# A table of slots for the side work of the x2 stage, an earlier second scale of w_out2, and a square moved one job back

## Chip, core and metric

The kernel runs on one core of a Trainium2 chip. The metric is the device time of one execution in microseconds (us). Engines: PE (TensorE, matrix products), DVE (VectorE), ACT (ScalarE), POOL (GpSimd), SP (SyncE, which here only issues DMAs; ACT issues some too).

## What is computed

```python
attn = masked softmax(q k^T / 8) v            # 4 x 8 heads, 576 tokens, 64 wide
x = attn as (2304, 512)
a, b = x @ w1, x @ w2                         # 512 -> 1024
x2 = ((a * b) @ w3) @ w_out                   # -> 512
h = x2 @ w_in                                 # 512 -> 2048
out = where(h > 0, h, exp(min(h, 0)) - 1) @ w_out2     # -> 512
```

All in float32 within the reference's tolerance; the kernel works with pairs of reduced-precision numbers (a high part and what it leaves over, the low part), so one product of the reference is three on PE.

## The kernel before

**Stages.** Attention, with the products a = x w1 and b = x w2 of the first three batches, is ordered by a planner and is the same in both kernels. Then, in program order: the a and b products of the last batch (`run_unit(ab_unit(...))`, L697); M = w3 w_out in eight units (`m_unit`, L1090); the **x2 stage**, x2 = M^T g (L1387); and the **last stage**, h and out (L1545 and L1495).

**Order.** Outside attention nothing is scheduled: each engine runs its instructions in the order in which the Python code emits them. An instruction that waits holds up all that stands behind it on its engine, and the same holds for the queues on which SP and ACT issue DMAs.

**Weights** come as 64-bit words in chunks of 128x2048 int32 (1 MB). A chunk's conversion (`conv_ops`) is: `top` (ACT, L337), `rest` (DVE, L347), `sign` (DVE, L351), `join` (DVE, L354), and for w_in and w_out2 a `square` with a sum per partition (ACT L370, or DVE L372) from which a power-of-two scale follows (`root`, L996 and L999). After `sign` the raw buffer is free and ACT issues the load of the chunk after next (L322). A w_out2 chunk (`wo_steps`) then is scaled (ACT, L1049), copied to its high half (ACT, L1050), and its low half is formed (POOL, L1051). These conversions are cut into `jobs`, and `run_jobs(k)` runs the next k of them at given places of the a·b, M, x2 and last stages.

**x2 stage.** Six passes x of 384 tokens, each of four blocks e: 24 blocks n = 4x + e of 24 matrix products each, into one of four PSUM banks. ACT evicts each block (L1425 for two passes, L1428 into one of two `x2s` buffers for the others, which SP stores) and squares it (L1225). All passes use the same eight split tiles `sl`. Right after the products of a pass's last block, n = 3, 7, 11, 15, 19, eight `split_g` are emitted, each an ACT copy (L326) and a DVE subtraction (L327), which refill them for the next pass; a refill waits for the products that read the old contents, and the first products of the next pass wait for the refill.

**Beside x2** a table `slot[n]`, run at the end of block n, holds the work on w_in, four pairs of chunks q: two conversions with square (`conv`), four sums of quarters on POOL (`both`, L1293), and then either seven products of the scaled quarters (`direct`, one ACT copy L1315 and one DVE subtraction L1318 each; q = 0, 1) or seven stores to DRAM (`all_out`, q = 2, 3). Before, pair q takes slots 5q to 5q+4, and the directs 5q+6 to 5q+9. The squares of a pair are added over partitions by a small PE product (`total`, L1229) at n = 5q+5, whose result DVE reads one block later (`w_scale`). Sums and scalings of x2's first two passes (`sums`, `high_b`, `low_b`) stand in passes 2 and 3.

**Last stage.** Three groups p of tokens by eight f: 24 steps s. A step has seven products (`product`, L1545) into two PSUM banks, whose results DVE and ACT combine (L1571, L1586) into four quarters, on which the ELU is formed and scaled by a column of `c_by` (L1477, L1482); between the products PE is filled with output products of the step before (L1495). For the first four steps the scale of w_out2 comes from half of its chunks; then all eight chunks are known, and a second maximum over partitions is taken through DRAM (`everywhere`: store, L1006, load into `mxb`, L1010, DVE reduction, L1013). In step 3 the maximum per partition is taken after product 4 (L1625), the load is emitted after product 6, and in step 4 after product 1 DVE reads it, computes `shift` and overwrites `c_by` (`h_scale`, L1260 to L1264).

## Time and profile before

| | |
|---|---|
| median of 3 runs | 1009.46 us (1007.98 to 1011.92) |
| profiled execution, its own time | 1010.8 us |
| its span, first to last instruction | 1009.0 us |
| busy: PE, DVE, ACT, POOL | 948.3, 760.4, 572.1, 408.7 us |
| mean granted PE clock | 0.986 |
| attention with its a·b products | 0 to about 430 us |
| last a·b products | to about 468 us |
| M | about 469 to 515 us |
| x2 stage | 514.9 to 637.5 us |
| last stage | 637.5 to 1009.0 us |

Busy shares are means over stages that have different limits. An idle stretch of PE is named by what released it; what it costs is read in the stage where it lies. The granted clock is that of PE, 1.00 being 2.4 GHz and 0.50 being 1.2 GHz.

### The profile page before, as it was taken

What the parts mean: (1) busy time and instruction counts of PE and PEld (TensorE: products, weight loads), DVE (VectorE), ACT (ScalarE), POOL (GpSimd) and SP (SyncE); (2) the same over time, 40 slices, a digit from 0 to 9 for tenths busy, and PEclk for the clock granted to TensorE, in tenths of its full rate; (3) what the DMA queues carried; (4) which work ended last, traced back from release to release, by engine and by line L of the source; (5) the groups of instructions that cost most, each with busy time, mean ns of one, the idle gap of its engine ahead of it and who ended that gap; (6) DMA issues with size and microseconds to landing.
All of it is one profiled execution on the core that took longest, in us unless ns stands there. A gap on an engine that the chain in (4) does not pass through costs nothing. (4 is left out here: it accounts for less than half of the span.)

```text
span 1009.0 us, 17082 instructions
## 1 busy us (share of the span) xinstructions
PE 948.3 (94%) x6086; PEld 697.7 (69%) x6086; DVE 760.4 (75%) x1445; ACT 572.1 (57%) x1003; POOL 408.7 (41%) x553
## 2 busy tenths in 40 slices
PE   7889999999899999998999979799899999999998
PEld 4456788978889988997888968454455555555554
DVE  6889886988677777586846985599769666776664
ACT  5777776887567765355456564666446223543333
POOL 3478774888688976252402322356300000000000
PEclk9999999999999999999999988999999999999999
DMA  8446655566999888775745556531001200010001
GB/s 265 150 130 164 154 154 157 150 175 167 201 176 204 180 165 161 223 255 176 267 132 172 187 192 202 204 106 34 17 1 44 82 1 1 1 63 1 1 1 63
DMA packets 158866, 130.58 MB, mean 129 GB/s; under 512 B 117340, under 2 KB 145468, under 8 KB 154172
## 3 DMA queue, kind: packets, MB, share of 16 engines
q1 hardware_dynamic: 154668, 99.82, 37.5%
q10 hardware_dynamic: 4112, 29.66, 8.9%
q8 instruction: 48, 0.79, 0.3%
q14 instruction: 38, 0.31, 0.1%
HBM read 80.68 MB, written 21.05 MB: 101 GB/s over the span
## 5 line engine op out<-in xcount | busy, mean ns | idle before, releaser
L697 PE MATMUL ab<-x,W 128*128 128x256 f32 (+1 forms) x1536 | 224.7, 299 | 5.5 <-DVE g L712 3.3
L697 PEld LDWEIGHTS ab<-x,W 128*128 128x128 f32 x1536 | 209.1, 190 | 14.0 <-issue 6.0
L1495 PE MATMUL o<-WO,gg 128*128 128x512 f16 x864 | 213.7, 380 | 0.0
L1545 PE MATMUL h<-so,WI 128*128 128x384 f16 x1008 | 193.2, 329 | 11.0 <-ACT th L1586 5.7
L1545 PEld LDWEIGHTS <-WI 128*128 128x128 f16 x1008 | 99.4, 99 | 96.0 <-issue 15.6
L1571 DVE SCALAR_TENSOR_TENSOR th<-h,back,th 128x384 f32<-128x384 f32 x168 | 100.9, 614 | 79.8 <-PE h L1545 74.7
L1495 PEld LDWEIGHTS <-gg 128*128 128x128 f16 x864 | 84.7, 98 | 85.2 <-issue 0.8
L537 DVE SCALAR_TENSOR_TENSOR e<-s,st,e 128x576 f32<-128x576 f32 x144 | 115.2, 809 | 24.5 <-ACT e L531 22.9
L1387 PE MATMUL x<-sl,M 128*128 128x384 f32 x576 | 110.6, 353 | 9.7 <-DVE sl L327 6.2
L513 DVE TENSOR_REDUCE st<-s 128x1 f32<-128x576 f32 x144 | 106.1, 750 | 17.7 <-PE s L503 10.1
L548 POOL TENSOR_TENSOR hl<-e,hl 128x512 f16<-128x512 f32 x94 | 110.1, 1172 | 21.4 <-ACT hl L544 17.1
L1387 PEld LDWEIGHTS x<-sl,M 128*128 128x128 f32 x576 | 106.3, 198 | 12.6 <-DVE sl L327 8.3
L1472 ACT ACTIVATE et<-et 128x384 f32<-128x384 f32 x96 | 49.1, 511 | 107.9 <-DVE et L1471 107.9
L1477 ACT ACTIVATE gg<-th,c_by 128x384 f16<-128x384 f32 x96 | 59.0, 614 | 81.1 <-DVE th L1475 81.1
L531 ACT ACTIVATE e<-s,st 128x576 f32<-128x576 f32 x108 | 78.4, 737 | 25.4 <-POOL st L521 16.4
L503 PE MATMUL s<-qk 128*128 128x288 f32 x480 | 82.7, 305 | 7.2 <-DVE e L537 6.3
L503 PEld LDWEIGHTS s<-qk 128*128 128x128 f32 x480 | 67.5, 188 | 16.0 <-issue 9.6
L544 ACT ACTIVATE hl<-e 128x576 f16<-128x576 f32 x94 | 63.2, 681 | 22.6 <-DMA pt<-hl 12.0
L1475 DVE SCALAR_TENSOR_TENSOR th<-et,th 128x384 f32<-128x384 f32 x96 | 56.5, 589 | 6.9 <-ACT et L1472 6.2
L1482 DVE SCALAR_TENSOR_TENSOR gg<-th,c_by,gg 128x384 f16<-128x384 f32 x96 | 60.2, 627 | 0.2 <-ACT gg L1477 0.2
L491 PE MATMUL s<-qkp 128*64 128x288 f32 x288 | 42.4, 429 | 7.1 <-ACT pt L589 3.7
L1090 PE MATMUL m<-WO,w 128*128 128x512 f32 x192 | 44.4, 391 | 3.0 <-DVE M L1100 1.9
(153 smaller groups left out, 1351.9 us busy)
## 6 DMA issues: line engine op xcount, KB each, us to landing
rqk<-in_qk SPq DMA_DIRECT2D x24, 576.0 KB
raw_wo<-in_wo ACTq DMA_DIRECT2D x12, 1024.0 KB
th<-g_dr SPq DMA_DIRECT2D x48, 192.0 KB
raw_w<-in_w SPq DMA_DIRECT2D x8, 1024.0 KB
raw_w<-in_w3t ACTq DMA_DIRECT2D x8, 1024.0 KB
raw_win<-in_win ACTq DMA_DIRECT2D x8, 1024.0 KB
vr<-in_v SPq DMA_DIRECT2D x16, 320.0 KB
g_dr<-g SPq DMA_DIRECT2D x16, 320.0 KB
```

The lines of the kernel that those rows point to most:

```text
L503: T.matmul(s[:, n, :HS], q, k[:, c:c + HS], start=(x == 0), stop=(x == len(ops) - 1))
L513: V.tensor_reduce(st[i][:, 0:1], sc[i][:, :, :HS], axis=AX.XY, op=ALU.max if plain else ALU.min, negate=plain)
L531: A.activation(et[i], sc[i][:, :, :HS], AF.Exp, bias=st[i][:, k:k + 1], scale=esc if plain else -1.0)
L537: V.scalar_tensor_tensor(et[i], sc[i][:, :, :HS], st[i][:, 1:2], et[i], op0=ALU.is_ge if p < NPL else ALU.is_le, op1=ALU.mult, accum_out=s ...
L544: A.activation(hl[i][:, :S], et[i].rearrange("p a b -> p (a b)"), AF.Copy)
L548: G.tensor_tensor(t[:, S + 64:], e[:, :512], t[:, :512], op=ALU.subtract)
L697: T.matmul(o[:, :w], wf[:, m, wx, kt, :], x[:, xx, :], start=(kt == 0 and k == 0), stop=(kt == NK - 1 and k == 2),)
L1387: T.matmul(o[:, :TB], M[:, f, mx, e * P:(e + 1) * P], gh[j, f][:, gx, :], start=(k == 0), stop=(k == 23),)
L1482: V.scalar_tensor_tensor(h[:, 1, :], x, c["by"], h[:, 0, :], op0=ALU.mult, op1=ALU.subtract)
L1495: T.matmul(po[j, t], dst["h"][:, gx, t * P:(t + 1) * P], WO[f // 2 % 4][:, f // 8, f % 2, wx, :], start=(first and k == 0), stop=(stop and ...
L1545: T.matmul(o[:, :TB], w[:, wx, kt, :], bs[k][:, kt, xx, :], start=(i == 0), stop=(i == 5),)
L1571: V.scalar_tensor_tensor(x, a, bk, b, op0=ALU.mult, op1=ALU.add)
```

## The change

Four edits.

1. A w_out2 chunk becomes five jobs instead of four: the square leaves the job of its join and starts the next, `size`; scaling and copying (`halves`) are a job of their own. The M stage runs `4 + f % 2` jobs per unit instead of 4.
2. The table beside x2 is rewritten. Pair q's two conversions and its sums stand at slots `t0[q]`; slots 2, 6, 10, 14 and 18 are empty. `directs` stand at 5, 7, 9 and 11; the stores of q = 2 and 3 at 13 and 17; `total` for pair q at n = 4, 8, 12, 16. `sums`, `high_b` and `low_b` go to slots 13 to 20. Of the last 20 w_out2 jobs, 10 run in slots 16 to 22 (before: 4 of 16 in slots 19 to 23).
3. In the last stage the remaining jobs run in steps 0 to 2, four per step (before: steps 0 to 3, three per step); `high_b` of the last two operands is emitted in step 0.
4. The second scale goes into columns of its own, `c_late`: maximum in step 2 after product 5, load emitted in step 3 after product 2, read and `h_scale` in step 3 after product 5 (for the other two groups in step 5).

```diff
         def size():
+            ops[7](raw_[:, c], A)
             root(two[:, c], raw_[:, c], LEAST, 2.0 ** -13)
...
-        return [
-            [ops[0], ops[1], lows], [ops[2]], [ops[3], lambda: ops[7](raw_[:, c], A)], [size, halves]
-        ]
+        return [[ops[0], ops[1]], [ops[2]], [ops[3]], [size], [halves] + [lows] * (q % 4 < 2)], lows
...
         if f < 6:
-            run_jobs(4)
+            run_jobs(4 + f % 2)
...
-        at = 5 * q
-        for i, ops in enumerate((ca, cb)):
-            for n, fns in enumerate(conv(keys[i], ops, i)):
-                slot[at + 2 * i + n] += fns
-        slot[at + 4].append(both)
+        def conv(i):
+            ops = (ca, cb)[i]
+            for fn in ops[:3]:
+                fn()
+            next_load(keys[i])
+            ops[3]()
...
+        def second():
+            size(0)
+            conv(1)
+            size(1)
+
+        t0 = ((0, 1, 3), (3, 4, 7), (8, 9, 11), (12, 13, 15))[q]
+        slot[t0[0]].append(call(conv, 0))
+        slot[t0[1]].append(second)
+        slot[t0[2]].append(both)
         if q > 1:
-            slot[at + 5].append(all_out)
+            slot[t0[2] + 2].append(all_out)
         else:
-            order = (1, 4, 6, 3, 0, 2, 5)
-            for n, k in enumerate(order):
-                slot[at + 6 + n // 2].append(call(direct, k))
-            slot[at + 10].append(lambda: behind.pop(0)())
+            slot[(5, 9)[q]].append(lambda: directs((1, 4, 6, 3)))
+            slot[(7, 11)[q]].insert(0, lambda: directs((0, 2, 5)))
...
-    for n in (19, 20, 22, 23):
-        slot[n].append(lambda: run_jobs(1))
+    for n, k in ((13, 0), (15, 1), (15, 2), (16, 3)):
+        slot[n].append(call(sums, k))
+    for k, n in enumerate((16, 17, 19)):
+        slot[n].append(call(high_b, k, 0))
+        slot[(17, 19, 20)[k]].insert(0, call(low_b, k, 0))
+    for n, k in ((16, 3), (17, 1), (19, 1), (20, 3), (21, 1), (22, 1)):
+        slot[n].append(call(run_jobs, k))
...
-            for q in range(4):
-                if n == 5 * q + 5:
-                    seen = total(o, wm[:, 2 * q:2 * q + 2])
-                    reads.append(lambda q=q, seen=seen: (seen(wg[:, q:q + 1], 1), w_scale(q)))
+            if n in (4, 8, 12, 16):
+                q = n // 4 - 1
+                seen = total(o, wm[:, 2 * q:2 * q + 2])
+                reads.append(lambda q=q, seen=seen: (seen(wg[:, q:q + 1], 1), w_scale(q)))
...
-            lows[q] = elu_low({"x": x, "name": q + "_" + nm, "dst": gg[q], "by": c_by[:, at:at + 1]})
+            lows[q] = elu_low({"x": x, "name": q + "_" + nm, "dst": gg[q], "by": (c_by if s < NH // 2 else c_late)[:, at:at + 1]})
...
-        run_jobs(int(s < NH // 2))
+        run_jobs(int(s < 3))
...
-        if s == NH // 2:
-            seen[1](o_two[:, 1:2])
...
+        if s == 3:
+            seen_o[0]()
...
+        if s == 2:
+            while behind:
+                behind.pop(0)()
+            V.tensor_reduce(o_two[:, 1:2], cols("wo_two", 8), axis=AX.X, op=ALU.max)
+            seen_o = everywhere(o_two[:, 1:2])
+        if s == 3:
+            seen_o[1](o_two[:, 1:2])
+            V.reciprocal(shift, o_two[:, 1:2])
+            V.tensor_scalar(shift, shift, o_two[:, 0:1], None, op0=ALU.mult)
+        if s in (3, 5):
+            h_scale((0,) if s == 3 else (1, 2), o_two[:, 1:2], c_late)
```

Three places in the programs show what moves.

**DVE ahead of the fourth split (n = 15), before.** `w_win_7300` is the second chunk of pair 2, with its square (`u_win_7298`); the `WI` rows are directs of pair 1, the `so` rows `low_b`, the rows on `sl` begin the split:

```order
L1214 SCALAR_TENSOR_TENSOR so_6724<-bq,x_to,so_6724 128x2x384
L1318 SCALAR_TENSOR_TENSOR WI_7255<-s_1_7151,w_to,WI_7255 128x2x256
L1318 SCALAR_TENSOR_TENSOR WI_7255<-w_win_6973,w_to,WI_7255 128x2x256
L351 TENSOR_SCALAR w_win_7300<-raw_win_7110 128x1024
L354 SCALAR_TENSOR_TENSOR w_win_7300<-u_win_7298,w_win_7300 128x1024
L372 SCALAR_TENSOR_TENSOR u_win_7298,wm<-w_win_7300 128x1024
L1214 SCALAR_TENSOR_TENSOR so_6725<-tq_6729,x_to,so_6725 128x2x384
L1318 SCALAR_TENSOR_TENSOR WI_7255<-w_win_6973,w_to,WI_7255 128x2x256
L327 TENSOR_TENSOR sl_6382<-th_6386,sl_6382 128x384
L327 TENSOR_TENSOR sl_6382<-th_6387,sl_6382 128x384
```

**DVE ahead of the same split, changed.** `w_win_7371` is the second chunk of pair 3; the row on `tq` is `sums(0)`, the rows up to `w_to` the scale of pair 2:

```order
L1230 TENSOR_REDUCE wg<-x_4_0_7284 128x1
L996 TENSOR_SCALAR w_two<-wg 128x1
L999 TENSOR_SCALAR w_two<-w_two 128x1
L1245 TENSOR_SCALAR w_to<-w_two 128x1
L1246 RECIPROCAL w_to<-w_to 128x1
L347 TENSOR_SCALAR w_win_7371<-raw_win_7182 128x1024
L351 TENSOR_SCALAR w_win_7371<-raw_win_7182 128x1024
L354 SCALAR_TENSOR_TENSOR w_win_7371<-u_win_7369,w_win_7371 128x1024
L372 SCALAR_TENSOR_TENSOR u_win_7369,wm<-w_win_7371 128x1024
L1202 TENSOR_TENSOR tq_6728<-bq 128x768
L327 TENSOR_TENSOR sl_6377<-th_6381,sl_6377 128x384
L327 TENSOR_TENSOR sl_6377<-th_6382,sl_6377 128x384
```

The directs of pair 1 and the two `so` rows no longer stand between a conversion and the split: pair 1's last directs come ahead of pair 3's conversions, the `so` rows after the split. Ahead of the third split (n = 11) the changed program has, since the second split, seven directs, two conversions and one square on DVE.

**ACT where the x2 stage ends, before.** `x_5_3` is the last block, `h_0_0` the first product of the last stage, `u_wo`, `w_wo` and `WO` belong to a w_out2 chunk, `so` are operands of the last stage:

```order
L1428 ACTIVATE x2s_3_7754<-x_5_3_7725 128x384
L1225 ACTIVATE x_5_2_7687,xm<-x_5_2_7687 128x384
L1049 ACTIVATE w_wo_7611<-w_wo_7611,wo_to 128x1024
L1050 ACTIVATE WO_2_7763<-w_wo_7611 128x2x512
L1225 ACTIVATE x_5_3_7725,xm<-x_5_3_7725 128x384
L1210 ACTIVATE so_7787<-tq_6730,x_to 128x2x384
L1210 ACTIVATE so_7789<-bq,x_to 128x2x384
L1586 ACTIVATE th_6386<-h_0_0_7799,back 128x384
```

**The same place, changed:**

```order
L1207 ACTIVATE so_7772<-bq,x_to 128x2x384
L1207 ACTIVATE so_7774<-tq_6728,x_to 128x2x384
L1446 ACTIVATE x2s_3_7776<-x_5_3_7747 128x384
L1223 ACTIVATE x_5_2_7716,xm<-x_5_2_7716 128x384
L1223 ACTIVATE x_5_3_7747,xm<-x_5_3_7747 128x384
L1596 ACTIVATE th_6381<-h_0_0_7811,back 128x384
L337 ACTIVATE u_wo_7819<-raw_wo_7508 128x1024
L1207 ACTIVATE so_7825<-tq_6730,x_to 128x2x384
```

The scaling and copying of a w_out2 chunk, and two `so` rows, no longer stand ahead of the eviction of product 0 (`th<-h_0_0`).

**DVE where the second scale is read, before** (`h_4_1` is step 4's product 1):

```order
L1571 SCALAR_TENSOR_TENSOR th_6387<-h_4_1_8409,back,th_6386 128x384
L1482 SCALAR_TENSOR_TENSOR gg_0_3_8397<-th_6391,c_by,gg_0_3_8397 128x384
L1013 TENSOR_REDUCE o_two<-mxb_8330 128x1
L1601 RECIPROCAL shift<-o_two 128x1
L1602 TENSOR_SCALAR shift<-shift,o_two 128x1
L1260 TENSOR_SCALAR out_by<-x_two,w_two 128x1
L1261 TENSOR_SCALAR out_by<-out_by,o_two 128x1
L1262 TENSOR_SCALAR up<-out_by 128x1
L1263 RECIPROCAL up<-up 128x1
L1264 TENSOR_SCALAR c_by<-wo_two,up 128x8
L1205 TENSOR_TENSOR tq_6729<-bq,tq_6728 128x768
L1571 SCALAR_TENSOR_TENSOR th_6390<-h_4_2_8436,back,th_6386 128x384
```

**The same, changed** (`h_3_6` is step 3's product 6):

```order
L1492 SCALAR_TENSOR_TENSOR gg_0_3_8329<-th_6385,c_by,gg_0_3_8329 128x384
L1013 TENSOR_REDUCE o_two<-mxb_8213 128x1
L1643 RECIPROCAL shift<-o_two 128x1
L1644 TENSOR_SCALAR shift<-shift,o_two 128x1
L1258 TENSOR_SCALAR out_by<-x_two,w_two 128x1
L1259 TENSOR_SCALAR out_by<-out_by,o_two 128x1
L1260 TENSOR_SCALAR up<-out_by 128x1
L1261 RECIPROCAL up<-up 128x1
L1262 TENSOR_SCALAR c_late<-wo_two,up 128x8
L1581 SCALAR_TENSOR_TENSOR th_6386<-h_3_6_8376,back,th_6384 128x384
L1485 SCALAR_TENSOR_TENSOR th_6387<-et_0_3_8355,th_6387 128x384
L1481 TENSOR_SCALAR et_0_3_8387<-th_6386 128x384
```

The read of `mxb` moved from step 4 after product 1 to step 3 ahead of product 6, and its result goes to `c_late`.

## Rows read from the trace of the kernel before

**Rows 1.** Windows, whole x2 stage and a quiet stretch: from:to, length, busy (count), clock, DMA.

```profile
515.00:637.00 122.00, 110.22 (x584) 107.06 (x583) 79.87 (x135) 68.22 (x148) 29.20 (x18) 0.93 0.57 184
...
760.00:880.00 120.00, 120.00 (x642) 62.68 (x641) 88.85 (x172) 48.53 (x89) 0.00 (x0) 1.00 0.07 27
```

**Rows 2.** Windows, the x2 stage pass by pass.

```profile
514.90:549.10 34.20, 34.18 (x195) 33.82 (x193) 16.77 (x31) 17.74 (x37) 8.70 (x6) 1.00 0.39 112
549.10:570.40 21.30, 19.35 (x101) 18.81 (x101) 18.70 (x29) 15.56 (x35) 7.83 (x4) 0.92 0.58 200
570.40:588.50 18.10, 17.09 (x96) 16.73 (x95) 14.05 (x26) 11.61 (x24) 0.00 (x0) 1.00 0.53 178
588.50:615.10 26.60, 19.91 (x99) 18.73 (x98) 20.14 (x28) 11.98 (x27) 9.27 (x6) 0.87 0.74 237
615.10:637.50 22.40, 20.30 (x98) 19.41 (x98) 10.72 (x25) 11.62 (x28) 3.40 (x3) 0.85 0.68 220
```

**Rows 3.** Timeline of PE, x2 stage: start, length, instruction, count [idle before <-releaser].

```profile
550.90 0.44 PE L1387 MATMUL x<-sl,M 128*128 128x384 f32 x1 [1.82 <-ACT sl L326]
...
595.74 1.33 PE L1387 MATMUL x<-sl,M 128*128 128x384 f32 x3 [3.90 <-DVE sl L327]
```

**Rows 4.** Timeline of DVE ahead of the fourth split.

```profile
594.07 5.98 DVE L327 TENSOR_TENSOR sl<-th,sl 128x384 fp32r<-128x384 f32 x8
```

**Rows 5.** Timeline of ACT: a square before the second split, an eviction before the fifth.

```profile
549.29 1.06 ACT L370 ACTIVATE u_win<-w_win 128x1024 f32<-128x1024 f32 x1 [2.13 <-DVE w_win L354]
...
614.86 0.49 ACT L1428 ACTIVATE x2s<-x 128x384 f32<-128x384 f32 x1 [6.26 <-DMA x_dr<-x2s]
```

**Rows 6.** Groups of instructions in the x2 stage, DVE: busy us, mean ns | idle before.

```profile
L327 DVE TENSOR_TENSOR sl<-th,sl 128x384 fp32r<-128x384 f32 x40 | 22.9, 643 | 13.8 <-ACT sl L326 13.8
...
L354 DVE SCALAR_TENSOR_TENSOR w_win<-u_win,w_win 128x1024 int32<-128x1024 int32 x8 | 10.2, 1273 | 5.1 <-ACT u_win L337 4.9
...
L1318 DVE SCALAR_TENSOR_TENSOR WI<-w_win,w_to,WI 128x512 f16<-128x512 f32 x6 | 7.6, 1259 | 1.7 <-ACT WI L1315 1.7
...
L347 DVE TENSOR_SCALAR w_win<-raw_win 128x1024 uint16<-128x1024 uint16 x8 | 7.0, 879 | 0.0
...
L351 DVE TENSOR_SCALAR w_win<-raw_win 128x1024 uint16<-128x1024 uint16 x8 | 6.1, 763 | 0.0
...
L1318 DVE SCALAR_TENSOR_TENSOR WI<-s,w_to,WI 128x512 f16<-128x512 f32 x8 | 5.9, 748 | 7.3 <-ACT WI L1315 7.3
...
L372 DVE SCALAR_TENSOR_TENSOR u_win<-w_win 128x1024 f32<-128x1024 f32 x4 | 4.9, 1224 | 0.1
```

**Rows 7.** Window and PE timeline, the first step of the last stage.

```profile
637.50:654.20 16.70, 9.48 (x47) 4.85 (x46) 12.23 (x24) 11.55 (x22) 7.53 (x10) 0.90 0.46 154
...
643.91 4.77 PE L1545 MATMUL h<-so,WI 128*128 128x384 f16 x18 [4.26 <-ACT th L1586]
```

**Rows 8.** Windows, steps 2, 4 and 5; timelines of PE and DVE in step 4.

```profile
669.30:683.90 14.60, 14.60 (x79) 7.63 (x78) 13.47 (x25) 10.30 (x19) 8.57 (x10) 1.00 0.42 146
698.50:714.60 16.10, 11.55 (x56) 5.57 (x55) 11.68 (x26) 5.59 (x14) 10.96 (x14) 0.94 0.16 38
714.60:730.00 15.40, 15.40 (x80) 7.92 (x79) 12.61 (x31) 8.22 (x18) 5.38 (x8) 0.95 0.00 0
...
711.63 1.14 PE L1545 MATMUL h<-so,WI 128*128 128x384 f16 x6 [3.57 <-DVE th L1571]
...
708.43 0.28 DVE L1013 TENSOR_REDUCE o_two<-mxb 128x1 f32<-128x128 f32 x1 [2.29 <-DMA mxb<-mx_dr]
```

**Rows 9.** Timelines of PE and ACT and a window, end of a·b and M stage.

```profile
460.18 7.59 PE L697 MATMUL ab<-x,W 128*128 128x256 f32 x48 [2.21 <-ACT a L705]
...
509.36 5.73 PE L1090 MATMUL m<-WO,w 128*128 128x512 f32 x24 [1.93 <-DVE M L1100]
...
506.54 1.06 ACT L370 ACTIVATE u_wo<-w_wo 128x1024 f32<-128x1024 f32 x1 [3.72 <-DVE w_wo L354]
...
460.20:463.00 2.80, 2.80 (x13) 2.80 (x14) 2.18 (x2) 0.97 (x1) 1.88 (x1) 0.50 0.33 120
```

More of the change, by code (lines that the diff above doesn't have):

```diff
@@ L1078, in attention_moe_moe2 @@
         jobs.append(nxt)
-        jobs.append(cs[3])
+        jobs += cs[3:]
     jobs[0] += jobs.pop(5)
@@ L1432, in attention_moe_moe2 @@
             unsized.append((x, e, o[:, :TB]))
-            if x == 2:
-                sums(e)
-            if x == 3 and e:
-                low_b(e - 1, 0)
-            if x == 3 and e < 3:
-                high_b(e, 0)
             if x == NB - 1 and e == NK - 1:
@@ L1453, in attention_moe_moe2 @@
     units += [hop.tile([P, 256], F32, name=f"wr{i}") for i in range(NUR)]
-    for k in (5, 6):
-        high_b(k, 0)
-    lowb = [(5, 0), (6, 0)]
+    lowb = []
     while nu[0] < NUR:
@@ L1528, in rescale @@
                 A.activation(o, o, AF.Copy, scale=shift)
-    late, later, highb = [], [], []
+    late, later, highb = [], [], [5, 6]
     steps = [(p, f) for p in range(NPR) for f in range(NH)]
@@ L1620, in attention_moe_moe2 @@
         lows["22"][0]()
-        run_jobs(int(s < NH // 2))
         if s == 0:
             seen = total(ph[0], xm[:, 8:24])
-        if s == NH // 2 - 1:
-            V.tensor_reduce(o_two[:, 1:2], cols("wo_two", 8), axis=AX.X, op=ALU.max)
-            seen = everywhere(o_two[:, 1:2])
-        if s == NH // 2 - 1 and behind:
-            behind.pop(0)()
         after(4)
@@ L1634, in attention_moe_moe2 @@
         lows["11"][2]()
+        run_jobs(int(s < 3))
+        if s == 2:
+            while behind:
+                behind.pop(0)()
+            V.tensor_reduce(o_two[:, 1:2], cols("wo_two", 8), axis=AX.X, op=ALU.max)
[6 more added lines that the diff above has]
+            h_scale((0,) if s == 3 else (1, 2), o_two[:, 1:2], c_late)
         after(5)
```

47 lines of the change are left out of this document (22 added, 25 removed).

## The prediction

> **What bounds the kernel now.** I read the windows by stage first. In a quiet stretch of the last stage PE is busy in all of its 120 us at clock 1.00; in the x2 stage it is busy in 110.22 of 122.00 us, at a mean clock of 0.93 [rows 1]. So PE bounds the kernel, and what can be won lies where PE stops, or runs at half clock after a stop. DVE, busy 79.87 us of those 122, and ACT, 68.22, are not the bound on the mean [rows 1]; they matter through the place at which PE waits for them.
>
> Next the x2 stage pass by pass [rows 2]. The first eight blocks take 34.20 us without a stop, 4.275 us a block, 17.1 us a pass of four. The four later passes take 21.30, 18.10, 26.60 and 22.40 us, so they lose 4.2, 1.0, 9.5 and 5.3, together **20.0 us**. Every one begins with PE waiting for the split tiles: the timeline names ACT's or DVE's `sl` row, with gaps such as 1.82 and 3.90 us [rows 3]. The half clock is the second part of the price: the passes with losses of 4.2, 9.5 and 5.3 have mean clocks of 0.92, 0.87 and 0.85, while the pass that lost 1.0 kept 1.00 [rows 2]. In the pass of 21.30 PE is idle 1.95 us, and the other 2.2 us are work at half clock.
>
> Then what held the splits, on the engines ahead of them. Before the second split ACT stood 2.13 us at a square whose join DVE had not done [rows 5]. Before the fourth, DVE was at conversions, directs and `low_b` until 594.07, and its eight subtractions then took 5.98 us [rows 4]. Before the fifth, ACT stood 6.26 us at an eviction whose `x2s` buffer was still being stored [rows 5].
>
> Last, three places outside x2. In step 0 of the last stage PE waits 4.26 us for ACT's eviction of product 0 [rows 7]. In step 4 it waits 3.57 us because DVE waits for the load of `mxb` [rows 8]. At the end of a·b it waits 2.21 us for an eviction on ACT, with half clock behind it, and before the last unit of M 1.93 us for one on DVE; there ACT had stood 3.72 us at a square [rows 9].
>
> **The change, part by part.**
>
> *The square one job later.* Nothing is added; ACT no longer stands at a join. In a·b this moves an eviction ahead of the scaling and copying of a chunk, and in M it lets ACT go on to the splits and evictions. At most it returns 2.2 us, plus half of the 2.80 us at clock 0.50 (1.4), plus 1.9, together 5.5 us [rows 9]; at least nothing, if the chunk conversions, which PE reaches earlier, then hold it in M. The gap on DVE may keep a part, so I take **3.5**. The chunk's last square now comes behind the last eviction of M, beside block 0; the four PSUM banks, three blocks of 4.275 us, cover it.
>
> *The table.* The empty slots 2, 6, 10, 14 and 18 put nothing ahead of a split but one block's eviction and square. The square of pair q on DVE is now three blocks ahead of its `total`, so PE stops no more there. Ahead of the fifth split the seven stores of pair 2 stand at slot 13 instead of just before it: the eviction that needs a buffer behind them is that of n = 16, with two blocks and an empty slot before the split. What is late next is DVE in the middle passes. From the second to the third split it gets four directs of sums and three of `w_win`, two conversions and a square: 4 x 0.748 + 3 x 1.259 + 2 x (0.879 + 0.763 + 1.273) + 1.224 = 13.8 us by the means [rows 6], and the split, up to 5.98 [rows 4]: 19.8 against a pass of 17.1, 2.7 late. If all seven directs cost 0.748 and the split 22.9/40 x 8 = 4.6 [rows 6], it is 12.3 + 4.6 = 16.9, not late. I take the middle, 1.4, and one stretch of half clock, 2.2 as read above. Up to the fourth split: four directs (4.5), two conversions and a square (7.1), and the split (6.0 or 4.6), 16.2 to 17.6, with one `sums` more; late by 0 to 1.5, I take 0.7. For the fifth and second splits together 0.7. That leaves 5 of the 20.0 us, so the table returns **15**; the ends are 20 (none late) and nearly nothing (rival 1).
>
> A row speaks of why the means differ: a direct of `w_win` takes 1.259 us, one of sums 0.748, at equal size [rows 6], and the eight subtractions took 5.98 us in the pass where POOL was busy for 9.27 us [rows 2, 4]. The Trainium skill, "SBUF — State Buffer", section "Who interferes with whom", says that DVE and GpSimd share one pair of ports under an exclusive lock, held for a whole instruction, so that a DVE instruction with two inputs in SBUF stands still until the GpSimd one has ended. The trace agrees in kind; by the rule taken to its end the table returns nearly nothing: the first rival.
>
> *The moved jobs.* Ten of the w_out2 jobs go into x2, where the last pass keeps them: after the fourth split DVE has only three `sums`, one chunk and one `low_b`. At the start of the last stage, the scaling and copying of a chunk and two `so` rows leave ACT's list ahead of product 0. The 4.26 us wait goes [rows 7]; one more conversion row (0.88 [rows 6]) is now on DVE there, and DVE, busy 12.23 of 16.70 us [rows 7], is next. I take **3.5**, between nothing and 5.
>
> *The second scale.* Steps 4 and 5 hold 56 + 80 PE products in 31.5 us; step 2 does 79 in 14.60, so 136 are worth 25.1 [rows 8]. The wait and its half clock thus cost 6.4 us. The load is now emitted four products after the store and read three products later, and a product is 14.60/7 = 2.1 us: 6.3 us from load to read. Before, DVE read with a 2.29 us wait right after the load [rows 8]. I take **6**, between 6.4 and nothing.
>
> *Sum.* 3.5 + 15 + 3.5 + 6 = 28 us. Against the profiled execution's own 1010.8 us (span 1009.0) this gives 982.8; the median of the runs, 1009.46, lies 1.3 us below that execution, so **981.5**, or 982. By the ends of the four terms the profiled time would lie between 974 and 1010; they will not all fall on one side.
>
> **The rivals.**
>
> 1. *DVE becomes the bound of the middle passes.* POOL's sums now fall into the same passes as the directs. POOL is busy 7.83 us in such a pass [rows 2]; if DVE stands still through all of it, the list is 12.3 + 4.6 + 7.8 = 24.7 against 17.1, 7.6 us late, twice, with 2.2 us of half clock each: 19.6 of the 20.0 us stay lost. The other terms make 13: 996. For it: 1.259 against 0.748 [rows 6]. Against it: not every DVE row waits, and before, DVE was free part of each pass (18.70 of 21.30 busy [rows 2]). Half of it gives 989.
>
> 2. *The scale is still late.* If SP, whose queue holds loads of w_in units between the store and the `mxb` load, is held by POOL, the read waits in step 3 as it did in step 4, and PE behind it: the 6 us stay, 987.5. The edit then does not do what it says. Against it: store and read are now seven products apart, before four.
>
> 3. *ACT held by its own load issues: slower.* Each conversion now issues its load on ACT before the next eviction and must wait for DVE's two rows on that raw buffer, 0.879 + 0.763 = 1.64 us, behind one more row, 1.27 [rows 6]: 2.9 us, ten times in x2. Should ACT fall four blocks (17.1 us) behind, PE has no bank left and stops each time: 29 us, and 2.2 of half clock each, 22. The x2 stage then takes 102.6 + 51 = 154 us instead of 122.6, 31 more; less the other 13, **1027**. Against it: ACT is busy only 17.74 of 34.20 us and at most 15.56 of 21.30 [rows 2], and it has an empty slot per pass to catch up.
>
> **How the numbers follow.** My forecast (974 to 988) has 0.55; rival 1 (988 to 999) 0.24; rival 2, which lies inside the range, 0.10; rival 3 0.03; several of these together, near no change, 0.05; better than all terms 0.03. No change means within 0.5%, 5 us, about what a measurement can tell here: faster 0.92, same 0.05, slower 0.03. For 8 in 10 the range reaches to 973 below, where nearly all waits vanish, and into rival 1 above, to 997.
>
> **What would show it.** Right: passes x = 2 to 5 at 17 to 19 us, clock 0.50 in one of them at most; the eviction of product 0 within 2.5 us of the x2 stage's end; no `mxb` wait on DVE in step 3 or 4; no square among ACT's longest waits. Wrong: PE gaps at n = 12 and n = 16 released by DVE's `sl` rows and above 3 us (rival 1); a DVE wait for `mxb` in step 3 (rival 2); gaps released by evictions, for want of a PSUM bank (rival 3).

## The result, and the profile after

| | before | changed |
|---|---|---|
| median (range), us | 1008.77 (1007.98 to 1011.92) | **993.20** (992.49 to 994.22) |
| ratio, 95% interval | | **0.9841**, 0.9817 to 0.9865 |
| profiled execution, its span | 1010.8, 1009.0 | 992.74, 991.0 |
| end of PE's last attention row | 411.36 | 408.62 |
| from there to the x2 stage (a·b and M) | 103.57 | 100.85 |
| x2 stage | 122.60 | 111.61 |
| last stage | 371.47 | 369.92 |
| busy: PE, DVE, ACT, POOL | 948.3, 760.4, 572.1, 408.7 | 943.4, 757.2, 572.3, 409.2 |

The kernel is faster by 15.6 us in the medians. The time lies 11 us above the forecast of 982: inside the range of 973 to 997, outside the forecast's own band of 974 to 988, and in the band that was given to rival 1. The spans differ by 18.0, but 2.7 of that is attention, which is the same program in both; in all fourteen traces of this study its end lies between 408.6 and 413.5 us, so each stage is compared by itself. The stages give 2.7 + 11.0 + 1.6 = 15.3 us, which is what the medians say.

Windows of the changed kernel; columns as in [rows 1]. The first three are the x2 stage, cut around its slow piece, the last two the start of the last stage:

```profile
509.47:563.20 53.73, 52.21 (x291) 51.33 (x290) 42.08 (x64) 36.53 (x72) 15.79 (x10) 0.97 0.59 166
563.20:582.00 18.80, 15.52 (x73) 14.69 (x72) 18.10 (x30) 11.68 (x27) 7.13 (x4) 0.82 0.67 216
582.00:621.08 39.08, 39.08 (x228) 38.85 (x227) 24.87 (x50) 27.40 (x59) 8.44 (x6) 1.00 0.81 272
621.08:640.15 19.07, 10.16 (x45) 4.88 (x45) 15.27 (x24) 10.28 (x21) 9.29 (x12) 0.80 0.29 86
640.15:646.00 5.85, 5.85 (x17) 2.54 (x17) 3.45 (x12) 4.73 (x9) 1.08 (x2) 0.50 0.10 27
```

PE no longer stops between 582 and 621 us, where two late splits lay before [rows 2]. What is left in x2 is the clock of 0.97, with 1.5 us idle, in the first window and of 0.82, with 3.3 us idle, in the second. Then, at the start of the last stage, a piece that was not there: 0.80 over 19.07 us and 0.50 over 5.85, that is 0.20 x 2 x 19.07 + 5.85, about 13.5 us at half clock, where the kernel before had a mean of 0.90 over 16.7 us [rows 7], about 3.3 us at half clock.

The timeline of the changed kernel around its first and third splits (start, duration, and in brackets the idle time before and who ended it):

```profile
528.46 0.80 PE L1405 MATMUL x<-sl,M 128*128 128x384 f32 x3 [0.76 <-DVE sl L327]
...
534.09 0.28 PE L1227 MATMUL x<-wm,ones 128*128 128x2 f32 x2
...
550.96 0.28 PE L1227 MATMUL x<-wm,ones 128*128 128x2 f32 x2
...
563.66 0.28 PE L1227 MATMUL x<-xm,ones 128*128 128x8 f32 x2
564.87 0.44 PE L1405 MATMUL x<-sl,M 128*128 128x384 f32 x1 [0.92 <-ACT sl L326]
567.07 0.96 PE L1405 MATMUL x<-sl,M 128*128 128x384 f32 x3 [1.75 <-DVE sl L327]
...
574.82 0.28 PE L1227 MATMUL x<-wm,ones 128*128 128x2 f32 x2
...
523.64 8.20 DVE L327 TENSOR_TENSOR sl<-th,sl 128x384 fp32r<-128x384 f32 x8
...
565.40 5.98 DVE L327 TENSOR_TENSOR sl<-th,sl 128x384 fp32r<-128x384 f32 x8
...
522.62 2.24 POOL L1291 TENSOR_TENSOR s<-w_win 128x512 f32<-128x512 f32 x1 [6.01 <-DVE w_win L354]
...
527.96 1.59 POOL L1291 TENSOR_TENSOR s<-w_win,s 128x512 f32<-128x512 f32 x1
```

The first split, clean before, is late now: DVE's eight subtractions take 8.20 us, with the four rows of POOL's `both(0)`, 522.62 to 529.55, beside them. A `total` on PE marks the end of blocks 4, 8, 11 and 12. From 534.09 to 550.96 four blocks run without a stop, 4.22 us each; four from 509.47 would at that pace end at 526.35, so block 4, done at 534.09, lost 3.5 us. Block 12, from 563.94 to 574.82, took 10.88 and lost 6.7: ACT's copies are late there, then DVE's subtractions, 5.98 us long. These are the whole loss: 24 blocks would be 101.3 us, and 111.61 is 10.3 more. The second, fourth and fifth splits lose nothing.

The same view at the start of the last stage:

```profile
623.76 1.14 PE L1555 MATMUL h<-so,WI 128*128 128x384 f16 x6 [0.56 <-ACT th L1596]
...
633.26 0.61 PE L1227 MATMUL h<-xm,ones 128*128 128x16 f32 x2 [4.91 <-DVE th L1581]
633.71 2.08 PE L1555 MATMUL h<-so,WI 128*128 128x384 f16 x6
...
640.15 2.08 PE L1555 MATMUL h<-so,WI 128*128 128x384 f16 x6 [1.55 <-DVE th L1581]
...
621.09 2.17 DVE L1211 SCALAR_TENSOR_TENSOR so<-bq,x_to,so 128x768 f16<-128x768 f32 x1 [5.26 <-ACT so L1207]
...
630.94 1.21 DVE L354 SCALAR_TENSOR_TENSOR w_wo<-u_wo,w_wo 128x1024 int32<-128x1024 int32 x1
632.08 1.13 DVE L1581 SCALAR_TENSOR_TENSOR th<-h,back,th 128x384 f32<-128x384 f32 x2
...
623.15 0.56 ACT L1596 ACTIVATE th<-h,back 128x384 f32<-128x384 f32 x1
```

ACT evicts product 0 at 623.15, 2.1 us behind x2's end, and PE's wait of 4.26 us [rows 7] is down to 0.56. But PE then stands 4.91 us in front of the row `total` behind product 4, and what it waits for is the end of a DVE list that runs from 621.09 without a stop of more than 0.3 us: four low parts `so`, the three conversion rows of a chunk (the last, L354, at 630.94), and the combines `th`. Some of its rows are long: the first `so` takes 2.17 us, beside a row of POOL that runs from 620.30 to 622.44, and the second 1.00. Product 5 starts 12.6 us behind x2's end, as before (650.16 less 637.53); from there PE is at half clock, and a product takes 2.08 us in place of 1.14.

The second scale, by SP's queue and DVE's list:

```profile
672.36 0.32 SPq L1006 DMA_DIRECT2D mx_dr<-o_two  x1
...
680.63 0.32 SPq L1010 DMA_DIRECT2D mxb<-mx_dr  x1
...
686.61 0.27 DVE L1013 TENSOR_REDUCE o_two<-mxb 128x1 f32<-128x128 f32 x1
```

Store at 672.36, load 8.27 us later, read 5.98 us after that with no wait; the gap of 3.57 us in step 4 [rows 8] is gone, and PE has no idle stretch after 646 us.

### The profile page after: what moved, and what is told of

The parts are those of the page before. It is cut to its first block, busy times and chain, and to the rows that moved or that the text cites. A ratio compares the mean times of both kernels' runs of the same rounds, so it can differ in the third digit from the quotient of the medians.

```text
span 991.0 us, 17082 instructions
## 1 busy us (share of the span) xinstructions
PE 943.4 (95%) x6086; PEld 692.9 (70%) x6086; DVE 757.2 (76%) x1445; ACT 572.3 (58%) x1003; POOL 409.2 (41%) x553
## 4 chain that ended last, share of the span: by engine, by line
PE 42%; DVE 4%; ACT 3%; issue 1%; DMA 1%; SPq 0%; DVEq 0%; ACTq 0%
PE o L1505 19%; PE h L1555 16%; PE x L1405 6%; DVE sl L327 1%; PE m L1087 1%; DVE w_win L354 0%; ACT WI L1313 0%; DVE WI L1316 0%; DVE w_wo L354 0%; ACT u_win L337 0%; ACT u_win L370 0%; DVE w_w L354 0%; DMA th<-g_dr 0%; DVE th L1581 0%; DVE M L1097 0%
## 5 line engine op out<-in xcount | busy, mean ns | idle before, releaser
L1405 PE MATMUL x<-sl,M 128*128 128x384 f32 x576 | 106.8, 345 | 4.8 <-DVE sl L327 3.9
L1405 PEld LDWEIGHTS x<-sl,M 128*128 128x128 f32 x576 | 103.6, 195 | 6.6 <-DVE sl L327 5.5
L1487 ACT ACTIVATE gg<-th,c_late 128x384 f16<-128x384 f32 x80 | 49.2, 615 | 74.0 <-DVE th L1485 73.8
L1485 DVE SCALAR_TENSOR_TENSOR th<-et,th 128x384 f32<-128x384 f32 x96 | 54.5, 567 | 6.1 <-ACT et L1482 5.7
L1492 DVE SCALAR_TENSOR_TENSOR gg<-th,c_late,gg 128x384 f16<-128x384 f32 x80 | 49.1, 614 | 0.2 <-ACT gg L1487 0.2
```

Of the source, the lines that this page charges most:

```text
L1405: T.matmul(o[:, :TB], M[:, f, mx, e * P:(e + 1) * P], gh[j, f][:, gx, :], start=(k == 0), stop=(k == 23),)
```

## Experiments

Each kernel is the changed one with the edit shown; a cut in an edit is marked by three dots. "x2" and "last" are the lengths of the stages in its trace, "last" from the first product of the last stage to the end. Ratios are to the kernel before, run on the same chip. Medians of different experiments are not to be compared, since the chips differ: the kernel before took 1007.48 us beside the mark and the kernels on loads, late square and jobs in step 0, and 1011.95 to 1012.78 beside the others.

### The mark

No edit: the changed kernel once more, as the mark for the others.

> The changed kernel itself once more, as the mark for the other runs, since attention, which is the same program in all of them, ended at 408.6 us in the one trace of the change and at 411.4 to 413.5 in others. Theory (attention scatters from execution to execution and the stages behind it do not): attention's end moves by up to 5 us, while from there on M starts after 53.6, takes 47.2, x2 111.6, the last stage 369.9, each within 0.5 us. Rival (the change also shortened attention): its end is at 408 to 409 us again.

Measured: 991.93 us, ratio 0.9842 (0.9814 to 0.9870). Attention ended at 409.32; a·b and M took 100.71, x2 110.53, the last stage 369.34. The stages repeat to 0.6 us except x2, which moved by 1.1; three kernels below that leave x2's program alone gave 110.38, 110.91 and 111.65. So what moves x2 by less than 1.3 us is not told from scatter. The ratio tells less still: only three kernels below have intervals clear of the mark's (0.9903, 0.9785 and 0.9761). What is said of the others rests on one trace each, read by stage. Attention's end was again early, and between 409.2 and 413.5 in the others, with the same program: scatter, as the theory has it.

### The square

```diff
-            ops[7](raw_[:, c], A)
             root(two[:, c], raw_[:, c], LEAST, 2.0 ** -13)
...
-[ops[2]], [ops[3]], [size]
+[ops[2]], [ops[3], lambda: ops[7](raw_[:, c], A)], [size]
```

> The changed kernel with one thing undone: the square of a w_out2 chunk stands in the job of its join again. Theory (the square alone held ACT in the a·b products and in M; the x2 stage began 5.5 us earlier because of it): the 5.5 us are lost again, x2 starts at about 515 us, the whole takes 998 to 999 us, and ACT shows waits of 2 us or more at a square on a join. Rival (the five jobs per chunk and the four or five jobs per M unit did it): x2 starts at 509 to 510 us and the time stays at 993. Either way the x2 stage itself keeps its 111.6 us within 1 us.

Measured: 998.06 us, ratio 0.9851 (0.9818 to 0.9883). By the trace a·b and M took 105.55 us, 4.8 more than in the mark, M alone 50.64 against 47.26; x2 111.04. Its timeline in M:

```profile
510.96 7.35 PE L1086 MATMUL m<-WO,w 128*128 128x512 f32 x24 [2.94 <-DVE M L1096]
...
508.14 1.06 ACT L370 ACTIVATE u_wo<-w_wo 128x1024 f32<-128x1024 f32 x1 [2.58 <-DVE w_wo L354]
```

ACT stands at the square until DVE's join, and PE behind it. The theory holds for the cause, in M: 3.4 us there, where twelve traces with the square moved lie between 47.2 and 47.4. The other 1.5 us, in a·b (54.91 against 53.45), are not told from scatter, since the next kernel, with the change's program there, took 54.84. The size expected was wrong by attention's scatter: against the kernel before, all of edit 1 is worth 2.7 us, not 5.5. With the square at its join this kernel's M is 4.4 us longer than before, so the new cut into jobs alone would have made M slower.

### The second scale

```diff
+        if s == 4:
+            seen_o[1](o_two[:, 1:2])
...
+        if s in (4, 5):
+            h_scale((0,) if s == 4 else (1, 2), o_two[:, 1:2], c_late)
         after(1)
...
-        if s == 3:
-            seen_o[0]()
         after(2)
...
+        if s == 3:
+            V.tensor_reduce(o_two[:, 1:2], cols("wo_two", 8), axis=AX.X, op=ALU.max)
+            seen_o = everywhere(o_two[:, 1:2])
         after(4)
...
         lows["22"][2]()
+        if s == 3:
+            seen_o[0]()
```

> The changed kernel with the second scale back at its old places: maximum in step 3 after product 4, load emitted after product 6, read in step 4 after product 1; the columns of its own stay. Theory (the edit gave back the wait of step 4 with its half clock, 6.4 us as read from the windows of before): 999 to 1000 us, a DVE wait of about 2.3 us for mxb and a PE gap of about 3.5 us in step 4. Rival (the jobs that now end in step 2 had already cleared the way, the places of store, load and read do not matter): 993, no gap in step 4.

Measured: 1000.05 us, ratio 0.9869 (0.9831 to 0.9907); last 376.64, 7.3 more than the mark.

```profile
689.84 0.32 SPq L1006 DMA_DIRECT2D mx_dr<-o_two  x1
...
698.43 0.32 SPq L1010 DMA_DIRECT2D mxb<-mx_dr  x1
...
702.94 0.29 DVE L1013 TENSOR_REDUCE o_two<-mxb 128x1 f32<-128x128 f32 x1 [5.44 <-DMA mxb<-mx_dr]
...
706.14 2.08 PE L1555 MATMUL h<-so,WI 128*128 128x384 f16 x6 [4.70 <-DVE th L1581]
```

The theory holds, and the wait is longer than before, 5.44 us on DVE and 4.70 on PE. The load starts 8.59 us behind the store, with two loads of `wr` between them in SP's queue, and the value is there 4.5 us later; in the kernel before the two were 8.0 and 4.1 (696.34, 704.36, 708.43), in another kernel below that reads the scale in step 4, 10.0 and 3.3. The changed kernel leaves 5.98 us for the 3.3 to 4.5: at least 1.5 us to spare.

### What holds the splits

Three kernels. POOL's sums of pairs 0 and 2 wait for the split:

```diff
+    hold = cols("hold")
...
             quarters()
+            if q in (0, 2):
+                G.tensor_scalar(hold, f32(gh[JS[q + 1], 7][:, 1, 0:1]), 0.0, 0.0, op0=ALU.mult, op1=ALU.add)
```

> The changed kernel, in which POOL's sums of pairs 0 and 2 wait until the last subtraction of the split beside them is done (one added POOL row of one element per pair that reads the last split tile). Theory (POOL's sums beside DVE's eight subtractions stretch them: 8.20 us at n = 3 where the kernel before took 3.84 without POOL beside it, 5.98 at n = 11): the first split's subtractions take 4 to 5 us, PE's two gaps of 0.76 us and the half clock behind them go (3.2 us), the third split's take 4.6 to 5 us and its gaps shrink by about 1; 988 to 990 us. Rival A (the subtractions follow ACT's copies or their loads): 8.2 and 6.0 us as before it, 993. Rival B (the sums, now later, meet the directs and conversions of the next pass, so that the second and fourth splits come late instead): first split clean, gaps at n = 8 or n = 16, 992 to 995.

Measured: 994.87 us, ratio 0.9823 (0.9788 to 0.9857); x2 109.95.

```profile
548.09 3.75 PE L1408 MATMUL x<-sl,M 128*128 128x384 f32 x20 [0.76 <-DVE sl L327]
...
586.91 5.39 PE L1408 MATMUL x<-sl,M 128*128 128x384 f32 x18 [1.35 <-ACT sl L326]
...
526.75 3.83 DVE L327 TENSOR_TENSOR sl<-th,sl 128x384 fp32r<-128x384 f32 x8
...
534.03 1.87 DVE L347 TENSOR_SCALAR w_win<-raw_win 128x1024 uint16<-128x1024 uint16 x1
...
566.40 3.83 DVE L327 TENSOR_TENSOR sl<-th,sl 128x384 fp32r<-128x384 f32 x8
```

The subtractions now take 3.83 us in both splits, the first split costs nothing, and PE's gaps at the third, together 3.27 us in the changed kernel, are 1.88. That POOL stretched them is shown; rival A is out. But the sums, later, stretch the conversions of the next pair (L347 1.87 us in place of 0.75), and PE stops 0.76 us at the second split and 1.35 at the fourth: rival B as well. Against the mark, pass by pass, 2.3 us are won at the first split and 2.5 at the third, 0.9 are lost at the second and 3.6 at the fourth: most of the gain is lost again. x2 is 0.4 to 1.7 us shorter than in the traces with its program as it was.

The loads one block later:

```diff
-            for fn in ops[:3]:
-                fn()
-            next_load(keys[i])
-            ops[3]()
+            for fn in ops[:4]:
+                fn()
...
+        for i in (0, 1):
+            slot[t0[i] + 1].insert(0, call(next_load, keys[i]))
```

> The changed kernel in which ACT issues each load of the chunk after next one block later, at the start of the next slot, instead of between a conversion's sign and its join. Theory (ACT stands at the issue until DVE has done the sign, about 3 us at 554 to 557 us and 1.2 at 562 us, so that block 10's eviction, and behind it the eight copies of the third split, come late): ACT's copies of the third split start where block 11's products end, PE's gap of 0.92 us on ACT's sl goes and the whole third split costs 1 to 2 us less with its half clock; x2 takes 109 to 110.5 us. Rival (DVE's own list, which ends at 565.4 us, sets the third split): the first gap goes but the next grows by as much, x2 stays at 111.6. A second rival: the loads, now later, hold up the conversions, x2 over 113.

Measured: 992.04 us, ratio 0.9844 (0.9817 to 0.9872); x2 109.68. The third split in the mark, then here:

```profile
564.67 0.44 PE L1405 MATMUL x<-sl,M 128*128 128x384 f32 x1 [1.17 <-ACT sl L326]
566.87 1.33 PE L1405 MATMUL x<-sl,M 128*128 128x384 f32 x3 [1.75 <-DVE sl L327]
```

```profile
565.97 0.45 PE L1405 MATMUL x<-sl,M 128*128 128x384 f32 x1 [0.60 <-ACT sl L326]
568.75 0.79 PE L1405 MATMUL x<-sl,M 128*128 128x384 f32 x3 [2.33 <-DVE sl L327]
```

ACT's gap shrinks from 1.17 to 0.60 and DVE's grows from 1.75 to 2.33: 2.92 and 2.93 together. The first rival holds; x2 is 0.7 us under the lowest trace with the program as it was, too little to tell.

The square of pair 2 behind the split:

```diff
             conv(1)
-            size(1)
+            if q != 2:
+                size(1)
...
+        if q == 2:
+            slot[t0[2]].append(call(size, 1))
...
-            if n in (4, 8, 12, 16):
-                q = n // 4 - 1
+            if n in (4, 8, 13, 16):
+                q = (n + 2) // 4 - 1
```

> The changed kernel in which DVE's square of pair 2 (1.30 us, the last row ahead of the third split) stands behind that split, and the small product that adds it over partitions one block later (n = 13). Theory (DVE's list ahead of the third split is too long by what the prediction reckoned): its subtractions start 1.3 us sooner, PE's gaps of together 3.27 us shrink by 1 to 1.3 and the half clock behind them by one stretch of 3.4 us: x2 109 to 110.3 us. Rival (ACT's copies, which also start late, at 564.30 us, set the third split): no shorter than 111.3.

Measured: 993.83 us, ratio 0.9859 (0.9832 to 0.9886); x2 110.46, inside the scatter.

```profile
568.01 0.80 PE L1408 MATMUL x<-sl,M 128*128 128x384 f32 x3 [0.73 <-DVE sl L327]
...
588.60 3.67 PE L1408 MATMUL x<-sl,M 128*128 128x384 f32 x17 [1.14 <-ACT sl L326]
```

DVE's gap falls from 1.75 to 0.73 as the theory had it, and 1.14 us come back at the fourth split, released by ACT. So at the third split ACT and DVE are both late by 1 to 2 us, and freeing one alone gives nothing that can be measured.

### Step 0

PE kept busy with products that nothing reads:

```diff
+    spare = ps_o.tile([P, 512], F32, tag="o", name="spare")
+    def busy(n):
+        for i in range(n):
+            T.matmul(spare[:, :TB], WI[0][:, 0, 0, 0, :], bs[0][:, 0, 0, :], start=(i == 0), stop=(i == n - 1))
...
+            busy(20)
             seen = total(ph[0], xm[:, 8:24])
...
+        if s == 0:
+            busy(6)
         quarter("12", product(6), u4)
...
+        if s == 1:
+            busy(8)
         o = product(0)
```

> The changed kernel with 34 extra PE products of 384 columns into a spare PSUM tile that nothing reads: 20 behind product 4 of step 0, 6 before its product 6, 8 before product 0 of step 1, where PE now idles 4.91, 0.71 and 1.55 us. Theory 1 (the half clock, 13.65 us of it behind PE's idle stretch in step 0, is the price: each of four products takes 2.08 to 2.10 us in place of 1.14, and the five o rows 2.34 in place of 1.24): the clock stays at 1.00 or is low in one short stretch, steps 0 and 1 take about 4 us less, 988 to 990 us. Theory 2 (DVE's list sets steps 0 and 1 by itself, PE's clock is hidden behind it): step 1's first product starts as late as now, 19.1 us behind the end of x2, and the time stays at 993 or is 1 to 2 us longer.

Measured: 993.87 us, ratio 0.9806 (0.9770 to 0.9841); last **365.85**, 3.5 to 4.1 under the two traces of the change, with the clock at 1.00 from 622.35 to 646. The four kernels with the extra products have 365.78 to 366.70, the five whose last stage is the change's 368.43 to 369.92.

```profile
629.47 3.41 PE L1478 MATMUL spare<-so,WI 128*128 128x384 f16 x20
633.70 0.39 PE L1227 MATMUL h<-xm,ones 128*128 128x16 f32 x2 [0.82 <-DVE th L1586]
...
639.89 1.14 PE L1560 MATMUL h<-so,WI 128*128 128x384 f16 x6 [1.56 <-DVE th L1586]
```

Theory 1 holds by the trace: the two groups do not overlap, and their means differ by 2.9 us. The runs' ratio cannot tell it from the mark. Step 0 takes 17.54 us (622.35 to 639.89) instead of 19.07, and the rest of the stage 348.31 instead of 350.85 and 350.29. Even so step 0 is 0.9 us longer than before (16.63, from 637.53 to 654.16): that much is DVE's list.

No job in step 0:

```diff
-        run_jobs(int(s < 3))
+        run_jobs(int(0 < s < 3))
...
-        run_jobs(int(s < 3))
+        run_jobs(2 * int(0 < s < 3))
```

> The changed kernel with no w_out2 job in step 0 of the last stage; steps 1 and 2 run six each instead of four. Theory (step 0 is bound by DVE's list between the end of x2 and the row total, in which the three conversion rows of the chunk, 0.74, 0.98 and 1.21 us, stand, and PE's idle stretch behind that list brings the half clock): PE's gap before total shrinks from 4.91 to about 2, the half clock from 13.65 us to at most 7, the last stage takes 366 to 367 us in place of 369.9. Rival (the list only moves: steps 1 and 2 are as full on DVE, and PE stops there): 370 us or more, with new gaps in steps 1 and 2.

Measured: 993.67 us, ratio 0.9854 (0.9827 to 0.9882); last 370.86.

```profile
635.86 0.61 PE L1227 MATMUL h<-xm,ones 128*128 128x16 f32 x2 [4.39 <-DVE th L1581]
...
632.41 1.15 DVE L1211 SCALAR_TENSOR_TENSOR so<-bq,x_to,so 128x768 f16<-128x768 f32 x1 [2.13 <-ACT so L1207]
...
631.14 0.42 ACT L1391 ACTIVATE WI<-wr 128x256 f16<-128x256 f32 x1 [2.44 <-POOL wr L1388]
...
630.62 1.49 POOL L1388 TENSOR_SCALAR wr<-wr,w_to 128x256 f32<-128x256 f32 x3 [13.62 <-DMA wr<-wi_dr]
```

Step 0 falls to 17.16 us, yet PE's gap before `total` only from 4.91 to 4.39: with the conversion rows gone, DVE waits 2.13 us for ACT's `so`, ACT 2.44 for POOL's scaling of the first `wr`, and POOL for the load of it, which lets POOL start 5.3 and 5.4 us behind x2's end in the two kernels. What was saved came back as new gaps in steps 1 and 2 (the rest of the stage takes 353.70). Two chains of about equal length end at that `total`.

Edit 3 and the places of edit 4 undone (three jobs per step, and the scale as in the kernel above that reads it in step 4):

```diff
-        jobs += cs
+        jobs += cs[:3] + [cs[3] + cs[4]]
...
-    for n, k in ((16, 3), (17, 1), (19, 1), (20, 3), (21, 1), (22, 1)):
-        slot[n].append(call(run_jobs, k))
+    for n in (19, 20, 22, 23):
+        slot[n].append(call(run_jobs, 1))
...
+    for k in (5, 6):
+        high_b(k, 0)
-    late, later, highb = [], [], [5, 6]
+    late, later, highb = [], [], []
...
-        run_jobs(int(s < 3))
+        run_jobs(int(s < 4))
...
```

> The changed kernel with edit 3 and the places of edit 4 undone, square and table kept: four of the late w_out2 jobs beside x2 (n = 19, 20, 22, 23), three per step in steps 0 to 3, the operands 5 and 6 copied before step 0, the second scale read in step 4. Theory (the moved jobs lost about 5 us where the prediction gave them 3.5: with the scale alone undone the last stage takes 376.6 us, before 371.5): the last stage takes 371 to 372 us, with one PE gap of about 4 us at product 2 of step 0, a half clock of one or two stretches of 3.4 us instead of 13.65, and the gap of about 3.5 us in step 4. Rival (the loss of steps 0 and 1 has nothing to do with the jobs: DVE's low parts and combines fill them anyway): 376 us or more. The x2 stage takes 110 to 112 us in either case.

Measured: 1002.05 us, ratio 0.9903 (0.9876 to 0.9930); last 377.49, step 0 18.88. The rival's number, but not by its cause:

```profile
628.76 5.33 PE L1557 MATMUL h<-so,WI 128*128 128x384 f16 x18 [5.73 <-ACT th L1598]
...
622.04 1.04 ACT L370 ACTIVATE u_wo<-w_wo 128x1024 f32<-128x1024 f32 x1
...
628.15 0.56 ACT L1598 ACTIVATE th<-h,back 128x384 f32<-128x384 f32 x1
```

With the square one job later, the job at the last block holds square, scaling and copying, 4.1 us of ACT's time (622.04 to 626.10, 0.7 of it a wait) ahead of product 0, and PE waits 5.73 us, not 4.26. So this is not the kernel before in step 0, and it does not tell edits 1 and 3 apart. It shows that with the square at its new place the moved jobs make no difference to the length of step 0 (18.88 against 19.07); behind it, PE's products take 1.14 us again; here its stop lies ahead of 18 products. Two more things can be read from it. The kernel of "The second scale" differs from this one by the moved jobs alone, and its last stage is 0.85 us shorter (376.64, step 0 19.08): with the square at its new place, the moved jobs are worth no more than that in these two traces. And x2 took 111.02 us with the jobs back at their places, so its gain over the kernel before is the table's, not theirs.

### Together

First all four of the held sums, the later loads, the later square and the extra products. Then the same without holding pair 0:

```diff
-            if q in (0, 2):
+            if q == 2:
```

Then the first again, without the later square.

> The changed kernel with four of the single changes together: POOL's sums of pairs 0 and 2 behind the split beside them, the loads issued one block later, DVE's square of pair 2 behind the third split, and the 34 extra PE products in steps 0 and 1. Theory (at the third split ACT and DVE are late by about the same, so that freeing one alone gave at most 1 us; freed together with POOL out of the way they give the sum): no PE gap over 0.5 us at the third split, x2 106 to 108 us, the last stage 366 as with the extra products alone, the whole 5 to 8 us under the change, ratio to before 0.976 to 0.979. Rival (what POOL does later only moves the stretched DVE rows into the next pass, and the second or fourth split is late in its place): x2 stays at 109.5 or more.

> As the kernel with all four, but POOL's sums of pair 0 are not held: only those of pair 2. Theory (holding pair 0's sums takes 3.2 us off the first split and gives some of it back at the second, where POOL then stretches the conversions of pair 1): the first split costs its 3.2 us again, the second none; x2 is 1 to 2 us longer than with all four. Rival (the second split loses with pair 0 held as much as the first gains): x2 within 0.5 us of the other.

> The kernel with all four changes, without the later square of pair 2 (whose total made PE wait 1.80 us for DVE at n = 13, and behind which ACT's copies of the fourth split came 2.74 us late): so the held sums, the later loads and the extra PE products. Theory (the late square alone brought the stop at n = 13 and the late fourth split, since it pushed DVE's list of that pass back by 2.3 us and ACT's square of block 11 waits for a read on that list): no gap at n = 13, the fourth split's gap on ACT under 1 us, x2 107 to 109.5 us, the last stage 366, the ratio to before 0.974 to 0.978. Rival (the held sums of pair 2, which stretch three directs to 4.2 us behind the third split, did it): the fourth split again costs 2 us or more, x2 110 or more, ratio 0.979 to 0.982.

| | median, us | ratio (95%) | x2 | last |
|---|---|---|---|---|
| all four | 991.24 | 0.9785 (0.9757 to 0.9812) | 112.06 | 366.70 |
| pair 0 not held | 993.77 | 0.9822 (0.9796 to 0.9848) | 113.32 | 365.78 |
| no later square | **989.56** | **0.9761** (0.9740 to 0.9781) | 111.48 | 366.56 |

All four:

```profile
576.18 0.38 PE L1227 MATMUL x<-wm,ones 128*128 128x2 f32 x2 [1.80 <-DVE u_win L372]
...
587.75 0.44 PE L1411 MATMUL x<-sl,M 128*128 128x384 f32 x1 [2.74 <-ACT sl L326]
...
573.82 2.29 DVE L372 SCALAR_TENSOR_TENSOR u_win<-w_win 128x1024 f32<-128x1024 f32 x1
```

The third split costs one gap of 0.59 us, and the later square, 2.29 us beside POOL, stops PE at n = 13; at the fourth split ACT's copies are 2.74 us late, behind a read on DVE's list: the rival holds. Holding pair 0 is worth 1.3 us, as the second of the three expectations had it: 2.3 won at the first split, 0.9 lost at the second, the other passes equal within 0.1. Without the later square the stop at n = 13 is gone, but the fourth split still loses some 6.6 us against the mark:

```profile
587.18 4.19 PE L1408 MATMUL x<-sl,M 128*128 128x384 f32 x15 [2.14 <-DVE sl L327]
...
586.58 8.18 DVE L327 TENSOR_TENSOR sl<-th,sl 128x384 fp32r<-128x384 f32 x8
...
587.95 1.72 POOL L1292 TENSOR_TENSOR s<-w_win 128x512 f32<-128x512 f32 x1 [9.52 <-DMA wi_dr<-s]
```

The gap of 2.14 us ends with the first subtraction, ahead of POOL's row at 587.95: it is DVE's list that ends late, at 586.58, and on it the rows L347 and L351 took 1.03 and 1.84 us beside the held sums of pair 2. So the pair that the rival named has a part. Then the subtractions are stretched to 8.18 us, with POOL's sums of pair 3 beside them, which nothing holds and which a DMA released 74.8 us behind x2's start, in the two traces of the change 83.8 and 79.5; three more gaps of 0.34 to 0.76 us follow. x2 is as long as the rival had it. By its ratio the last kernel is faster than the mark and than the second of the three; from the first it is not clear. Its trace shows some 3 us of that, in the last stage, and x2 no shorter than in the mark. Where the rest comes from the trace does not show; it is of the slowest of the five runs, 993.04 us.

## Why the prediction was right, and where its steps were off

Faster, and by three of the four terms; the forecast of 982 was too good by 11 us. The time falls in rival 1's band, 988 to 999, but not by rival 1's account, which left x2 all but unchanged: the table returned 11.0 us. One term came out below its lower end, and that the sum still fell in the wide range is in part luck, since nothing in the forecast allowed for that loss. By term:

| term | taken (ends) | measured |
|---|---|---|
| square | 3.5 (0 to 5.5) | 2.7: a·b 57.31 to 53.60, M 46.26 to 47.25 |
| table | 15 (0 to 20) | 11.0 (12.1 in the mark) |
| moved jobs | 3.5 (0 to 5) | **-5.0**, all that the last stage lost, whatever the edit |
| second scale | 6 (0 to 6.4) | 6.5: the stage behind step 0 from 354.84 to 348.31 at full clock |

Of the 12.7 us between 28 and 15.3 the moved jobs are 8.5 and the table 4.0.

**Square.** Right for a·b, where the early eviction returned the 3.6 us that were read from the gap and its half clock. Wrong for M, which was to return up to 1.9 us and became 1.0 longer: the wait ahead of its last unit is 1.21 us, and two waits of 0.55 and 0.66 are new, one for POOL and one for DVE. "No square among ACT's longest waits" was wrong too: three squares still wait 2.0 to 2.9 us for their join, two in a·b and one in M.

**Table.** Right for the second, fourth and fifth splits and in naming the third as late. Mis-sized by 4 us: the first split was thought clean, and lost 3.5 (2.0 in six of the ten traces in which POOL's sums run beside it, the mark's among them: the two stops of 0.76 us are the same there, but no half clock stands behind them). The reason is rival 1's mechanism at a place where the prediction did not look: it followed DVE's list and did not ask when POOL's `both(0)`, whose inputs come two blocks earlier by the new table, would now run. The third was taken at 3.6 and lost 6.7, since ACT too was late there: pass x = 3 took about 23.5 us, where 17 to 19 were named as the sign of being right. So two passes had half clock in this trace, one of them x = 1, which the sign left out. Rival 1's sign, gaps above 3 us at n = 12 and at n = 16, came only in part: three gaps of together 3.27 us at n = 12, 0.92 of it ACT's, and none at n = 16. Rival 3's waits at load issues exist; taking them away gained nothing that can be told from scatter.

**Moved jobs: the step that failed.** "The 4.26 us wait goes", and it did; that DVE "is next" was right as well, but its list was not laid end to end from x2's end. Done so it fills the 12.2 us up to `total`, about the instant at which the kernel before reached it (12.39), so the wait's removal could return nothing. The row that it gained ahead of `total` is also the join L354, 1.21 us, not the 0.88 that was taken. The term's lower end was nothing; the stage lost 2.4 us in step 0 and 2.5 behind it. PE's stop moved from ahead of 18 products that could run back to back [rows 7] to ahead of products that each wait for DVE, and there the half clock stayed for some 13.5 us. That the clock is the price of most of the loss is shown by the extra products (3.5 to 4.1 us back against the two traces of the change, 2.9 by the means of the two groups). Which of the edits made the list so long is open: with the jobs back at their old places, step 0 was as long (18.88), held by the square on ACT, so the loss is not shown to be the moved jobs' own.

**Second scale.** Right, and for the reason given: 5.98 us from load to read, 6.3 in the prediction. Undoing it alone cost 6.7 to 7.3 us of the last stage.

## What to carry to other kernels

When a wait goes, lay the list of the engine that is next end to end from the moment the wait began: if it fills the same time, nothing comes back, and the stop may land where PE has less ready behind it. An idle engine is not free to use: in this kernel POOL's sums stretched DVE's subtractions and conversions beside them, so a table that moves DVE's work must say when POOL's runs. And compare stages, not spans, when a part that nobody changed scatters by 5 us.
